# A gated mix of a state-space convolution and segment attention: second half with one PSUM tile per role, transfers on SyncE, reciprocals from SBUF to SBUF, and eight unread products a unit

## The chip, the cores and the metric

The program runs on one core of a Trainium2 chip. The metric is device microseconds (us) of one execution. The engines are TensorE (PE, matmuls; PEld, its weight loads), VectorE (DVE), ScalarE (ACT), GpSimd (POOL) and SyncE (SP, which issues transfers). Each takes its instructions in order and they wait for each other by semaphores. A transfer (DMA) is issued by SP, ACT or POOL, and the issuing engine waits in its own queue until what the transfer needs is ready.

## The reference

Inputs: `A_u` (1 x 2048 x 448), the parameters of a diagonal state-space model for 448 channels with 256 states, four 448 x 448 weights, 16 values `beta`, and a gate vector.

```python
x = A_u
g = sigmoid((x * gate_w).sum(-1, keepdims=True))
# branch a: K[d, l] = 2 Re sum_n C[d,n] exp(A[d,n] dt[d] l); y = causal convolution of u with K by FFT
a = irfft(rfft(u_t, 2 * L) * rfft(K, 2 * L))[:L] + u * D_skip
# branch b: 16 heads of 28, four segments of 512 positions
for s in range(4):
    p = softmax(qs @ ks.T * scale + causal_mask)
    a_dot = p @ vs
    a_mem = (phi(qs) @ M) / (phi(qs) @ z + 1e-6)      # memory of the earlier segments
    o = sigmoid(beta) * a_mem + (1 - sigmoid(beta)) * a_dot
    M, z = M + phi(ks).T @ vs, z + phi(ks).sum()
b = concat(o) @ wo
return g * a + (1 - g) * b
```

All of it is float32.

## The kernel before

**Two halves.** The first half (to about 443 us) makes the convolution's kernel and the projections. It leaves in DRAM the queries and keys of each segment and head group (`QD`, `KD`), the values (`VD`), the memory's numerators and denominators (`AM`, `DM`) and the transform of the input (`GU`). The change does not touch it. The second half, `second_half` at L1219, does the attention and the rest of the convolution together.

**The unit.** A unit `i` is one segment and one group of four heads, 16 in all. It has six rounds (`r` in L1280). Each round steps several generators by one, in an order written out by hand that PE, ACT and DVE keep:

- `ahead`: one step of `maxima` (L982) of unit `i + 2`: PE multiplies queries with keys, 32 rows a head, into a PSUM tile; DVE takes the row maxima of it (two to four reads of 128 to 512 columns). After six steps the maxima are transposed on PE (`ps_m`), negated on ACT (`mn`) and sent by POOL's queue into row 28 of the query tile.
- `w`: one step of `weigh` (L1018) of unit `i`: the logits with keys on the rows, from three products each, into a PSUM tile; ACT takes the exp of it into `PT`. At the end POOL zeroes what lies above the diagonal (`affine_select`, L1045).
- `vals` in round 1: `values` (L1047) of unit `i - 1`: 32 products of `PT` with `V` into the tile `pv`, which ACT copies to `pvs`. Row 28 of each head's 32 is the sum of the weights.
- `cv`, 0.68 of a step per round in units 1 to 12: `convolve` (L568). For each of 16 blocks `m` it goes through `transform` (PE, ACT copies to `ks`, ACT issues two transfers that swap halves of `ks`), `product` (PE, then DVE multiplies twice into `pr`) and `back` (PE, ACT copies to `bs`, ACT issues the store to `BB`).
- `ends`: one step of `seg_end` (L1160) in the rounds other than 1, two a round in all six rounds of unit 13. It starts in round 1 of units 4, 8 and 12, for the segment before.

**The segment end.** `norm` (L1105) collects the sums of the weights from `pvs` into `dn` (four transfers from POOL), `inverse` (L1068) takes the reciprocal on DVE, splits it in a high and a low part `rs`, writes them to a DRAM tile `RD` and reads them back into eight rows of `r8`, both from POOL's queue. Later a product with `k.sel` spreads each row over the 32 partitions of a head, and DVE multiplies `pvs` with it. `recall` (L1086) does the same for the denominators of the memory (`dm`, rows 32 to 40 of `r8`) and scales `am`. `skip` (L1131) loads a block of the input as `xt`, and POOL multiplies it by `dbc` (D_skip) and by `gt` (the gate). The output products of a segment are four groups of four matmuls (`out_mm`), added to `xt` by DVE and stored to `TB`.

**PSUM.** L1587 gives the second half one tile `m`, one `pv`, and three tiles of `a`, each of 128 x 1024. Maxima, weights and every step of the convolution take the next of the three in turn. A new user of a tile waits on PE until the engine that read the last contents is done.

**Unread products.** `turn_over` (L1236) multiplies constants, 128 x 128 by 128 x 512 in bf16, into `pv`. Nobody reads the result. There are three in each of the four rounds ahead of unit 0 and in the six of unit 0, and one beside each of the eight `last` steps of units 14 and 15 (the convolution's final transform, L666).

**Transfers.** `k.dma` (L1412) issues from SP, `k.adma` from ACT, `k.pdma` from POOL. `k.ldma` is `k.dma` placed behind the latest load of `gu`. SP's transfers are ordered by a planner; PE's matmuls keep the order of the program, and `k.dve` and `k.sca` chain DVE's and ACT's.

Of the kernel before, what the change touches and what calls it, by code (L numbers as in the profile page):

```python
# [27 lines left out]
SEG = 512  # L28
# [512 lines left out]
def transform_k(nc, k, fp):  # L541


    k2 = k.kb.rearrange("p b q -> p (b q)")
    gkv = k.GK.rearrange("k r n d -> (k r) n d")
    for i in range(8):
        gs = fp.tile([128, 4, 4, 112], F32, tag="gs", name="gs", bufs=4)
        pts = [k.ps("a") for jj in range(2)]
        for b in range(2):
            o = (32 * b + 4 * i) * 112  # L550
            for j in range(4):
                r = slice(32 * j, 32 * j + 32)
# [12 lines left out]
        yield  # L565


def convolve(nc, k, fp):  # L568
# [31 lines left out]
    def transform(m):  # L600
# [4 lines left out]
        for a in range(2):  # L605
            k.adma(x[a, :, 1], x[1 - a, :, 0])

# [7 lines left out]
    def back(m):  # L615

        pt = k.ps("a")
        w, x = cb[m // 2][:, m % 2], pr.pop(m)
# [27 lines left out]
def finish(nc, k, fp):  # L646
# [19 lines left out]
    def last(wc):  # L666
        ws = slice(2 * wc, 2 * wc + 2)
        py = k.ps("a")
        for w in range(2):
# [277 lines left out]
def attend(nc, k, ap):  # L947
# [34 lines left out]
    def maxima(i):  # L982
# [4 lines left out]
        for b, hp in MSTEPS:  # L987
            pt = k.ps("a")
            for t, o, n in PLACES[b]:
# [28 lines left out]
    def weigh(i):  # L1018
# [3 lines left out]
        for b, hp in STEPS:  # L1022
            pt = k.ps("a")
            for kt, o, n in PLACES[b]:
# [42 lines left out]

    def inverse(x, rows, h0, h1, dst, queue):  # L1068


        f = 16 * (h1 - h0)
        rc = ap.tile([128, 64], F32, tag="rc", name="rc", bufs=1)
        rs = ap.tile([128, 2, 64], F32R, tag="rs", name="rs", bufs=1)
        v.reciprocal(rc[:, :f], x)
        v.tensor_copy(rs[:, 0, :f], rc[:, :f])
        v.tensor_tensor(rs[:, 1, :f], rc[:, :f], rs[:, 0, :f], ALU.subtract)
        rd = k.dr.tile([2, 4, 32 * f], F32, tag=f"RD{f}", name="RD", bufs=2)
        queue(rd.rearrange("b j (i f) -> (j i) b f", f=f), rs[:, :, :f].bitcast(F32))
        queue(
            dst[rows : rows + 8, h0:h1].rearrange("p h q -> p (h q)").bitcast(F32),  # L1080
            rd.rearrange("b j q -> (b j) q"),
        )

    am, r8 = {}, {}

    def recall(s):  # L1086

        am[s] = ap.tile([128, 4, SEG], F32, tag="am", name="am", bufs=1)
        k.ldma(am[s], k.AM[:, :, s - 1].rearrange("h p q -> p h q"))
        dn = ap.tile([128, 64], F32, tag="dm", name="dm", bufs=1)  # L1090
        k.ldma(dn, k.DM[s - 1].rearrange("j h (i f) -> (j h i) f", f=64))
        r8[s] = ap.tile([40, 4, SEG], F32R, tag="r8", name="r8", bufs=1)
        for _ in range(2):
            yield
        v.tensor_scalar(dn, dn, 1e-6, None, ALU.add)
        inverse(dn, 32, 0, 4, r8[s], k.pdma)
        for _ in range(3):
            yield
# [6 lines left out]
    def norm(s, h0, h1, queue):  # L1105

        pvs = pvss[s]
        f = 16 * (h1 - h0)
        dn = ap.tile([128, 64], F32, tag="dn", name="dn", bufs=1)
        for j in range(4):  # L1110
            queue(
                dn[32 * j : 32 * j + 32, :f],
                pvs[32 * j + 28 : 32 * j + 29, h0:h1].rearrange("o h q -> o (h q)").rearrange("o (i f) -> o i f", f=f),
            )
        if s == 0:
            r8[s] = ap.tile([40, 4, SEG], F32R, tag="r8", name="r8", bufs=1)
        for _ in range(2):
            yield
        inverse(dn[:, :f], 0, h0, h1, r8[s], queue)
        for _ in range(3):  # L1120
            yield
        for hg in range(h0, h1):
            o = pvs[:, hg]
# [7 lines left out]
    def skip(s, t):  # L1131

        i = 4 * s + t
        xt = ap.tile([128, D], F32, tag="xt", name="xt", bufs=4)
        k.ldma(xt, k.u[128 * i : 128 * i + 128])
        k.pin(nc.gpsimd.tensor_tensor(xt, xt, k.dbc, ALU.mult))
        k.pin(nc.gpsimd.tensor_scalar(xt, xt, k.gt[:, i : i + 1], None, ALU.mult))
        return xt

# [6 lines left out]
    def skip_last():  # L1146

        for t in range(4):
            xt = skip(3, t)
            i = 12 + t  # L1150
            k.dma(k.TB[128 * i : 128 * i + 128], xt)

    def out_mm(s, t, po, hgs):
# [32 lines left out]
    def last_end(step, vals):  # L1186
# [7 lines left out]
        for _ in range(2):  # L1194
            pt = k.ps("a")
            pos += [pt[:, 0, :D], pt[:, 1, :D]]
# [22 lines left out]
def second_half(nc, k, ap, tp, fp, fin):  # L1219
# [53 lines left out]
    n = 0  # L1273
    for i in range(16):
# [69 lines left out]
def gated_mix(ctx, tc, k):  # L1344
# [297 lines left out]
```

## Time and profile before

| what | value |
|---|---|
| three runs | 857.24, 858.96, 859.09 us, median 858.96 |
| the profiled execution | 861.14 us |
| its span, first to last instruction | 859.4 us |
| mean granted clock of TensorE | 0.899 |
| bytes moved, read and written in DRAM | 88.77 and 60.63 MB, 174 GB/s |

The granted clock is the share of TensorE's full clock that the throttle let through. In this trace it is either 1.0 or 0.5 at a time, and a figure between these is a mean over a stretch. Busy time of PE runs from the first start to the modelled end of pipelined matmuls, so it is an upper bound of what PE did. A row of waits names the engine and tile that waited, the one that ended the wait, the sum in us, the number of times and the longest. A row of a group gives line, engine, operation, tiles (out<-in), shapes and count, then busy us and mean ns, then idle time ahead of it. Most engine work goes through helpers, so the lines L1354 and L1400 stand for many operations and the tile names tell them apart.

### The profile page before, as it was taken

Reading aid. Unit: us, or ns where it says so; the run is one execution under the profiler, and the core shown is the slowest. Engines: PE = TensorE matmul, PEld = TensorE weight load, DVE = VectorE, ACT = ScalarE, POOL = GpSimd, SP = SyncE. Lnnn points to the kernel's source line nnn. Section 1 sums busy time; section 2 is a strip of 40 time slices with the busy share of each in tenths; the row PEclk is TensorE's granted clock in tenths of the full one; section 3 lists DMA queues with packets and bytes.
Section 4 is the critical chain, followed back from the end, with each engine's and each line's share of the span. In section 5 each row is a group of like instructions: output and inputs, shape, how many; then the busy total and the mean of one; then the engine's idle time right before and its main releaser. Section 6 shows DMA issues by size and latency. Waiting matters only on the chain.

```text
span 859.4 us, 18898 instructions
## 1 busy us (share of the span) xinstructions
PE 721.2 (84%) x7583; PEld 393.7 (46%) x7583; DVE 579.7 (67%) x1139; ACT 510.1 (59%) x610; POOL 194.1 (23%) x233
## 2 busy tenths in 40 slices
PE   1687988998889989899989888889887798747897
PEld 1364655764447645466544433334333344313343
DVE  8878678777787777886668745456475657524475
ACT  4876889799997989989852333434243334411220
POOL 5324111001110111101100211171117116711110
PEclk9998999999999989999989867869886797858699
DMA  9347853334633246323569976686558467562684
GB/s 242 93 111 235 241 184 110 98 106 161 207 125 96 93 152 207 132 83 114 195 233 338 358 200 211 221 262 241 179 167 297 129 223 245 196 221 95 162 268 132
DMA packets 90337, 158.22 MB, mean 184 GB/s; under 512 B 20626, under 2 KB 58186, under 8 KB 90202
## 3 DMA queue, kind: packets, MB, share of 16 engines
q1 hardware_dynamic: 78618, 138.74, 50.6%
q10 hardware_dynamic: 9984, 16.52, 5.4%
q0 software_dynamic: 1648, 1.76, 0.7%
q8 instruction: 60, 0.98, 0.5%
q14 instruction: 27, 0.22, 0.1%
HBM read 88.77 MB, written 60.63 MB: 174 GB/s over the span
## 4 chain that ended last, share of the span: by engine, by line
PE 45%; DVE 17%; ACT 16%; DMA 10%; issue 8%; POOL 2%; SPq 1%; ACTq 1%; DVEq 0%; POOLq 0%
PE ps_a L1400 16%; PE ps_m L1400 14%; ACT cs L1354 7%; PE ps_pv L1400 6%; PE ps_arg L1400 4%; DVE jk L1354 4%; PE ps_k L1400 3%; DVE Y L396 3%; ACT L1354 2%; DMA r<-RD 2%; PE ps_m L1403 2%; DVE Y L397 2%; DMA w<-WD 1%; DVE X L392 1%; DMA RD<-rs 1%
## 5 line engine op out<-in xcount | busy, mean ns | idle before, releaser
L1354 ACT ACTIVATE PT<-ps_a 128x1024 f32<-128x1024 f32 (+1 forms) x96 | 84.1, 881 | 155.8 <-PE ps_a L1400 145.7
L1354 DVE CUSTOM_DVE_ANT_0 jk<-ps_a,mk 128x512 f32<-128x512 f32 (+3 forms) x256 | 125.3, 490 | 73.3 <-PE ps_a L1400 64.8
L358 POOL TENSOR_TENSOR EX<-EX,cab 128x1024 f32<-128x1024 f32 x28 | 54.0, 1929 | 307.4 <-ACT EX L1354 286.0
L1354 ACT ACTIVATE cs<-ps_arg 128x1024 f32<-128x1024 f32 x111 | 107.3, 1020 | 2.4 <-DVE Y L397 2.1
L1400 PE MATMUL ps_a<-qu,ku 32*128 32x512 f32 (+3 forms) x768 | 98.6, 379 | 10.0 <-DVE mx L1354 8.1
L1400 PE MATMUL ps_m<-xh,w 112*128 112x512 f32 x256 | 92.8, 412 | 1.9 <-DMA w<-WD 1.9
L1045 POOL TENSOR_SCALAR_AFFINE_SELECT PT<-PT 128x256 f32<-128x256 f32 (+1 forms) x96 | 46.8, 491 | 200.8 <-ACT PT L1354 199.8
L392 DVE TENSOR_TENSOR X<-EX,cs 128x1024 f32<-128x1024 f32 x56 | 70.2, 1254 | 24.3 <-ACT cs L1354 24.1
L1400 PEld LDWEIGHTS ps_a<-qu,ku 32*128 32x128 f32 x768 | 66.5, 206 | 22.3 <-DVE mx L1354 14.3
L1400 PE MATMUL ps_k<-Y,X 128*32 128x64 f32 x3584 | 64.1, 226 | 11.8 <-DVE Y L397 11.8
L1400 PEld LDWEIGHTS ps_k<-Y,X 128*32 128x32 f32 x3584 | 54.9, 113 | 37.4 <-DVE Y L397 20.2
L396 DVE TENSOR_TENSOR Y<-EY,cs 128x1024 f32<-128x1024 f32 x56 | 70.0, 1251 | 0.0
L1354 ACT ACTIVATE cs<-cs,bhp 128x1024 f32<-128x1024 f32 x56 | 64.4, 1151 | 1.8
L1400 PE MATMUL ps_a<-ku,qu 32*128 32x512 f32 (+3 forms) x256 | 49.5, 418 | 14.2 <-DVE mx L1354 7.1
L398 DVE SCALAR_TENSOR_TENSOR Y<-EY,cs 128x512 f32<-128x512 f32 x56 | 39.1, 699 | 31.2 <-ACT cs L1354 30.1
L1354 ACT ACTIVATE EY<-ps_arg 128x1024 f32<-128x1024 f32 x52 | 53.1, 1031 | 10.1 <-PE ps_arg L1400 9.0
L1400 PEld LDWEIGHTS ps_m<-xh,w 112*128 112x128 f32 x256 | 48.0, 188 | 21.0 <-issue 7.9
L1400 PEld LDWEIGHTS ps_a<-ku,qu 32*128 32x128 f32 x256 | 23.7, 198 | 71.9 <-issue 28.8
L1400 PE MATMUL ps_pv<-PT,V 128*32 128x128 f32 (+3 forms) x512 | 51.8, 560 | 0.0
L1400 PE MATMUL ps_arg<-ct,lh 64*128 64x512 bf16 x224 | 43.5, 386 | 8.2 <-ACT cs L1354 5.7
L1400 PE MATMUL ps_m<-xl,w 112*128 112x512 f32 x128 | 50.2, 392 | 0.0
L1354 DVE TENSOR_TENSOR pr<-ps_a,ks 128x896 f32<-128x896 f32 x32 | 33.4, 1085 | 18.8 <-PE ps_a L1400 11.3
(210 smaller groups left out, 1288.6 us busy)
## 6 DMA issues: line engine op xcount, KB each, us to landing
w<-WD SPq DMA_DIRECT2D x32, 448.0 KB, 4.2
qu<-QD SPq DMA_DIRECT2D x16, 512.0 KB, 6.0
ku<-KD SPq DMA_DIRECT2D x16, 512.0 KB, 7.5
GU<-gs SPq DMA_DIRECT2D x32, 224.0 KB, 3.8
GK<-gs SPq DMA_DIRECT2D x8, 896.0 KB, 5.0
gk<-GK SPq DMA_DIRECT2D x16, 448.0 KB, 4.2
gu<-GU SPq DMA_DIRECT2D x16, 448.0 KB, 6.7
ks<-ks ACTq DMA_DIRECT2D x32, 224.0 KB, 4.1
```

The costliest lines, as they stand in the source:

```text
L358: nc.gpsimd.tensor_tensor(o, o, cab, ALU.mult)
L392: v.tensor_tensor(X, ex, t[:, :, 0], ALU.mult)
L396: v.tensor_tensor(Y[:, :, :, :32], lo, y[:, :, :, ::-1], ALU.mult)
L397: v.tensor_tensor(Y[:, 0, :, 32:], ey[:, :, 32:], y[:, 0], ALU.mult)
L398: v.scalar_tensor_tensor(Y[:, 1, :, 32:], ey[:, :, 32:], -1.0, y[:, 1], ALU.mult, ALU.mult)
L1045: nc.gpsimd.affine_select(sl, sl, pat, ALU.is_ge, 0.0, base=0, channel_multiplier=-1)
L1354: x = op(*args, **kw)
L1400: tc.keep_in_program_order(nc.tensor.matmul(*args, **kw))
L1403: tc.keep_in_program_order(nc.tensor.transpose(*args))
```

## The change

- **PSUM**: the three tiles `a` are replaced by one `mx` (maxima), one `w` (weights) and one `c` (convolution). The transform ahead of unit 0 uses `w` and `c`; `last` alternates `c` and `mx`; the final projection takes `w` and `mx`.
- **Queues**: the swap of `ks` and the store of `bs` move from ACT's queue to SP's. `dn` and all transfers of the reciprocals move from POOL's queue to SP's.
- **Reciprocals**: `inverse` has no DRAM tile. Each of the eight rows of `r8` is written by one transfer from 32 partitions of `rs`.
- **Segment end**: the loads and collections of `norm` and `recall` are stepped ahead, the multiplication of `xt` by `gt` goes to ACT and follows its load by a step, ahead of POOL's by `dbc`; `am` is loaded after the last use of its tile and its products come with the last two output groups. In unit 13 two steps a round are taken only from round 2 on. The same work for the last segment (`skip_last`) is spread over units 10 and 11.
- **Unread products**: in units 1 to 15 there is one ahead of rounds 0 and 2 and two ahead of rounds 3, 4 and 5.

```diff
-        pts = [k.ps("a") for jj in range(2)]
+        pts = [k.ps(t) for t in ("w", "c")]
...
-            k.adma(x[a, :, 1], x[1 - a, :, 0])
+            k.dma(x[a, :, 1], x[1 - a, :, 0])
...
-        k.adma(k.BB[4 * m : 4 * m + 4].rearrange("(i s) r n d -> (s r n) i d", i=2), bs)
+        k.dma(k.BB[4 * m : 4 * m + 4].rearrange("(i s) r n d -> (s r n) i d", i=2), bs)
...
-        py = k.ps("a")
+        py = k.ps(("c", "mx")[wc % 2])
...
-            pt = k.ps("a")
+            pt = k.ps("mx")
...
-            pt = k.ps("a")
+            pt = k.ps("w")
...
+    def inverse(x, rows, dst):
+        rc = ap.tile([128, 64], F32, tag="rc", name="rc", bufs=2)
+        rs = ap.tile([128, 2, 64], F32R, tag="rs", name="rs", bufs=2)
+        v.reciprocal(rc, x)
+        v.tensor_copy(rs[:, 0], rc)
+        v.tensor_tensor(rs[:, 1], rc, rs[:, 0], ALU.subtract)
+        for b in range(2):
+            for j in range(4):
+                o = rows + 4 * b + j
+                k.dma(
+                    dst[o : o + 1].rearrange("o h (i f) -> o (h i) f", f=64).bitcast(F32),
+                    rs[32 * j : 32 * j + 32, b].bitcast(F32),
+                )
...
     def recall(s):
+        dn = ap.tile([128, 64], F32, tag="dm", name="dm", bufs=1)
+        k.ldma(dn, k.DM[s - 1].rearrange("j h (i f) -> (j h i) f", f=64))
+        yield
+        v.tensor_scalar(dn, dn, 1e-6, None, ALU.add)
+        inverse(dn, 32, r8[s - 1])
+        yield
         am[s] = ap.tile([128, 4, SEG], F32, tag="am", name="am", bufs=1)
         k.ldma(am[s], k.AM[:, :, s - 1].rearrange("h p q -> p h q"))
+        yield
         for hg in range(4):
             pb = k.ps("m")
-            k.mm(pb, k.sel[32:40], r8[s][32:40, hg], start=True, stop=True)
+            k.mm(pb, k.sel[32:40], r8[s - 1][32:40, hg], start=True, stop=True)
...
+    def scaled(s, t, xt):
+        i = 4 * s + t
+        act(xt, xt, AF.Copy, scale=k.gt[:, i : i + 1])
         k.pin(nc.gpsimd.tensor_tensor(xt, xt, k.dbc, ALU.mult))
-        k.pin(nc.gpsimd.tensor_scalar(xt, xt, k.gt[:, i : i + 1], None, ALU.mult))
...
     def seg_end(s):
         xts = [skip(s, t) for t in range(4)]
-        yield from norm(s, 0, 4, k.pdma)
-        memory = recall(s + 1)
+        sums, memory = norm(s), recall(s + 1)
+        next(sums)
+        next(memory)
+        yield
+        for t in range(2):
+            scaled(s, t, xts[t])
+        yield
+        for t in range(2, 4):
+            scaled(s, t, xts[t])
+        yield
+        next(sums)
+        yield
+        next(memory)
+        yield
+        yield
+        for _ in range(4):
+            next(sums)
+            yield
+        next(memory)
         for t in range(4):
             po = k.ps("m")
             out_mm(s, t, po[:, :D], range(4))
             store(s, t, po[:, :D], xts[t])
-            next(memory)
+            if t > 1:
+                next(memory)
             yield
         yield from memory
...
             else:
+                if r != 1:
+                    turn_over(1 if r < 3 else 2)
                 step(ahead)
                 step(w)
...
-                for _ in range(2 if i == 13 else 1):
+                for _ in range(2 if i == 13 and r > 1 else 1):
...
-            if i == 11 and r == 2:
-                k.skip_last()
+            if i == 10 and r == 2:
+                skips = k.skip_last()
+            if i == 10 and r > 2 or i == 11 and r < 3:
+                step(skips)
...
-            {"m": ([128, 512], 1), "a": ([128, 2, 512], 3), "pv": ([128, 512], 1)},
+            {"m": ([128, 512], 1), "pv": ([128, 512], 1)} | {t: ([128, 2, 512], 1) for t in ("mx", "w", "c")},
```

More of the change, by code (lines that the diff above doesn't have):

```diff
@@ L588, in second @@
     def second(m, x):
-        pt = k.ps("a")
+        pt = k.ps("c")
         w = cf[m // 2]
@@ L615, in back @@
     def back(m):
-        pt = k.ps("a")
+        pt = k.ps("c")
         w, x = cb[m // 2][:, m % 2], pr.pop(m)
@@ L1022, in weigh @@
         for b, hp in STEPS:
-            pt = k.ps("a")
+            pt = k.ps("w")
             for kt, o, n in PLACES[b]:
@@ L1066, in values @@
         yield
[L1068 to L1082, printed above, removed]
+    def inverse(x, rows, dst):
[11 more added lines that the diff above has]
+                )
@@ L1091, in recall @@
[L1091 to L1098, printed above, removed]
+        yield
         for hg in range(4):
             pb = k.ps("m")
-            k.mm(pb, k.sel[32:40], r8[s][32:40, hg], start=True, stop=True)
+            k.mm(pb, k.sel[32:40], r8[s - 1][32:40, hg], start=True, stop=True)
@@ L1102, in recall, with norm @@
             v.scalar_tensor_tensor(am[s][:, hg], am[s][:, hg], k.gh[:, hg : hg + 1], pb, ALU.mult, ALU.mult)
             yield
-    def norm(s, h0, h1, queue):
+    def norm(s):
         pvs = pvss[s]
-        f = 16 * (h1 - h0)
         dn = ap.tile([128, 64], F32, tag="dn", name="dn", bufs=1)
         for j in range(4):
-            queue(
-                dn[32 * j : 32 * j + 32, :f],
-                pvs[32 * j + 28 : 32 * j + 29, h0:h1].rearrange("o h q -> o (h q)").rearrange("o (i f) -> o i f", f=f),
-            )
[L1115 to L1122, printed above, removed]
+            k.dma(
+                dn[32 * j : 32 * j + 32],
+                pvs[32 * j + 28 : 32 * j + 29].rearrange("o h q -> o (h q)").rearrange("o (i f) -> o i f", f=64),
+            )
+        r8[s] = ap.tile([40, 4, SEG], F32R, tag="r8", name="r8", bufs=1)
+        yield
+        inverse(dn, 0, r8[s])
+        yield
+        for hg in range(4):
@@ L1135, in skip @@
         k.ldma(xt, k.u[128 * i : 128 * i + 128])
+        return xt
+    def scaled(s, t, xt):
+        i = 4 * s + t
+        act(xt, xt, AF.Copy, scale=k.gt[:, i : i + 1])
         k.pin(nc.gpsimd.tensor_tensor(xt, xt, k.dbc, ALU.mult))
-        k.pin(nc.gpsimd.tensor_scalar(xt, xt, k.gt[:, i : i + 1], None, ALU.mult))
-        return xt
     def store(s, t, po, xt):
@@ L1146, in skip_last @@
     def skip_last():
-        for t in range(4):
-            xt = skip(3, t)
+        xts = [skip(3, t) for t in range(4)]
+        yield
+        for t, xt in enumerate(xts):
+            scaled(3, t, xt)
             i = 12 + t
             k.dma(k.TB[128 * i : 128 * i + 128], xt)
+            yield
     def out_mm(s, t, po, hgs):
@@ L1161, in seg_end @@
         xts = [skip(s, t) for t in range(4)]
-        yield from norm(s, 0, 4, k.pdma)
-        memory = recall(s + 1)
+        sums, memory = norm(s), recall(s + 1)
[9 more added lines that the diff above has]
+        next(sums)
+        yield
+        next(memory)
+        yield
+        yield
+        for _ in range(4):
+            next(sums)
+            yield
+        next(memory)
         for t in range(4):
@@ L1193, in last_end @@
             yds.append(yd)
-        for _ in range(2):
-            pt = k.ps("a")
+        for t in ("w", "mx"):
+            pt = k.ps(t)
             pos += [pt[:, 0, :D], pt[:, 1, :D]]
```

2 lines of the change are left out of this document (removed).

## The prediction

> **What bounds the kernel now.** I read the page first, then the stretches of the second half, then who made TensorE (PE) wait there.
>
> ```profile
> span 859.4 us, 18898 instructions
> PE 721.2 (84%) x7583; PEld 393.7 (46%) x7583; DVE 579.7 (67%) x1139; ACT 510.1 (59%) x610; POOL 194.1 (23%) x233
> PEclk9998999999999989999989867869886797858699
> PE 45%; DVE 17%; ACT 16%; DMA 10%; issue 8%; POOL 2%; SPq 1%; ACTq 1%; DVEq 0%; POOLq 0%
> ```
>
> PE is the busiest engine and holds the largest share of the chain that ended last. Its granted clock is near full in the left half of the slices and falls to 5 to 8 tenths in the right half, which is what the change touches. The next view cuts that half at the value products (the `pv` groups, one per unit): units 1 to 4, 5 to 8, 9 to 12, unit 13 and the end. Columns: length, busy time of PE, PEld, DVE, ACT and POOL, granted clock, DMA share, GB/s.
>
> ```profile
> 491.60:576.40 84.80, 71.23 (x558) 31.82 (x556) 43.68 (x141) 33.86 (x43) 27.21 (x42) 0.72 0.69 217
> 576.40:665.40 89.00, 76.71 (x610) 34.68 (x612) 52.80 (x161) 33.79 (x43) 28.58 (x44) 0.85 0.67 225
> 665.40:764.40 99.00, 76.16 (x603) 35.36 (x605) 55.21 (x161) 33.08 (x42) 39.11 (x52) 0.79 0.64 215
> 764.40:801.90 37.50, 27.86 (x135) 13.76 (x139) 17.22 (x46) 6.03 (x8) 4.46 (x9) 0.77 0.36 108
> 801.90:859.40 57.50, 51.23 (x294) 21.28 (x294) 33.94 (x45) 11.38 (x15) 6.33 (x13) 0.92 0.64 187
> ```
>
> Two losses show. First, PE is busy but at a reduced clock. If busy time scales with the clock, each stage loses busy x (1 - clock): 71.23 x 0.28 = 19.9, 76.71 x 0.15 = 11.5, 76.16 x 0.21 = 16.0, 27.86 x 0.23 = 6.4 and 51.23 x 0.08 = 4.1, together 57.9 us. Second, PE idles: 84.8 - 71.2 = 13.6 us in the first stage, and much more in the third and fourth. Who it waits for, in total, times, longest:
>
> ```profile
> PE ps_m L1400 <- DMA r<-RD: 20.5, 3, 13.0
> PE ps_a L1400 <- DVE mx L1354: 13.0, 17, 3.5
> PE ps_a L1400 <- DVE pr L1354: 6.2, 5, 2.2
> PE ps_a L1400 <- ACT PT L1354: 3.9, 6, 0.9
> PE ps_m L1400 <- DVE pvs L1354: 3.2, 2, 2.3
> ```
>
> The largest is the transfer of the reciprocals at the segment ends. Around its longest case POOL did this:
>
> ```profile
> 739.64 1.15 POOL L1136 TENSOR_TENSOR xt<-xt,dbc 128x448 f32<-128x448 f32 x1
> ...
> 749.63 1.40 POOL L1137 TENSOR_SCALAR xt<-xt,gt 128x448 f32<-128x448 f32 x1
> 750.99 0.64 POOL L1045 TENSOR_SCALAR_AFFINE_SELECT PT<-PT 128x512 f32<-128x512 f32 x1
> 751.57 0.80 POOL L1078 DMA_DIRECT2D RD<-rs  x1
> 756.79 0.53 POOL L1079 DMA_DIRECT2D r<-RD  x1 [4.42 <-DMA RD<-rs]
> ```
>
> POOL is in order. From 739.64 to 751.03 the multiplications by `dbc` and `gt` stood ahead of the issue at L1078, and then two transfers ran one after the other through DRAM, while PE did nothing for 13.0 us.
>
> **Term A, reciprocals: -18.** The change issues these transfers from SyncE (SP), past POOL's work, and drops the DRAM leg. The landing times (KB each, us to landing) bound the new chain:
>
> ```profile
> RD<-rs POOLq DMA_DIRECT2D x6, 64.0 KB, 3.0
> r<-RD POOLq DMA_DIRECT2D x6, 64.0 KB, 4.6
> dn<-pvs POOLq DMA_DIRECT2D x12, 8.0 KB, 5.5
> xt<-in_A_u SPq DMA_DIRECT2D x16, 224.0 KB, 6.3
> ```
>
> Before: 3.0 + 4.6 plus two issues plus POOL's delay. After: eight issues of one row each and one landing like `dn<-pvs`, the nearest (small, SBUF to SBUF): with an issue at the 0.53 us of L1079 above, 8 x 0.53 + 5.5 = 9.7 us. At least three rounds lie between reciprocal and use; a round is 84.8 / 24 = 3.5 us, so the cover is 10.5. It fits narrowly. At segment 2 the old program stepped twice a round, leaving half of that cover; the new one doubles only from round 2 on. I take 18 of the 20.5; bounds 0 and -20.5.
>
> **Term B, clock: -29.** Eight unread products of the full array per unit are added, in the rounds other than 1. Does that hold the clock? These rows decide (columns as in the stage view):
>
> ```profile
> 474.70:478.10 3.40, 2.48 (x14) 1.01 (x15) 2.96 (x14) 0.58 (x1) 0.00 (x0) 1.00 1.00 402
> 560.00:563.40 3.40, 2.23 (x22) 1.44 (x18) 3.33 (x9) 1.77 (x2) 3.37 (x5) 1.00 0.98 309
> 570.30:573.70 3.40, 3.40 (x24) 1.15 (x16) 1.40 (x4) 1.22 (x2) 3.36 (x4) 0.50 0.94 269
> 589.00:615.00 26.00, 25.93 (x185) 12.13 (x185) 16.48 (x47) 8.38 (x12) 5.20 (x10) 1.00 0.68 235
> 684.00:716.00 32.00, 31.52 (x235) 14.71 (x239) 20.55 (x57) 11.96 (x16) 6.67 (x12) 1.00 0.71 234
> 815.00:855.00 40.00, 38.98 (x223) 16.36 (x219) 27.18 (x38) 7.84 (x11) 4.53 (x9) 1.00 0.70 217
> ```
>
> The three long stretches keep 1.00: there, full-array output products or the last transform mix with the attention products, and PE is busy 97% and more. The first two rows are full-clock stretches with PE 66 to 73% busy, and in both the clock falls right behind them. At 570.3 PE is 100% busy at 0.50: in the cold state the narrow attention and 64x64 products alone don't bring the clock back. So work that fills the gaps with the full array should both delay the fall and hasten the return. But unit 0 already has three products a round, and the first row lies there. I take half of the 57.9; bounds 0 and -50.
>
> The Trainium skill, "TensorE: Matmul & The Clock Gate", section "Why this matters for your kernels", says that the clock falls when PE idles for more than about 3 us. This case's rows disagree: the stretches at 474.7 and 560.0 held 0.9 and 1.2 us of idle in all. By that rule products put into short gaps would bring nothing, which is the first rival.
>
> **Term C, price of the products: +19.** Fifteen units times eight is 120. In unit 0 three in a row moved the next group by this much, at full clock and then at half:
>
> ```profile
> 470.09 0.81 PE L1400 MATMUL ps_pv<-wz 128*128 128x512 bf16 x3
> 470.83 0.50 PE L1400 MATMUL ps_a<-ku,qu 32*128 32x384 f32 x4
> ...
> 478.00 1.39 PE L1400 MATMUL ps_pv<-wz 128*128 128x512 bf16 x3
> 479.31 0.79 PE L1400 MATMUL ps_a<-qu,ku 32*128 32x512 f32 x2
> ```
>
> That is 0.74 / 3 = 0.25 us each at full clock and 1.31 / 3 = 0.44 at half, so 30 us in all, or 52 if everything were cold. Nothing hides it in the dense stretches: 16 products in units 14 and 15 (4.0 us) and, over 26 + 32 = 58 us of about 21 us a unit, 22 more (5.5 us). The other 82 (20.5 us) stand ahead of the maxima, where PE waits for the reads of the last maxima (13.0 us above); I call half hidden, so 4.0 + 5.5 + 10 = 19. Bounds 9.5 and 52. A product also takes the `pv` tile, so the one of round 2 waits for ACT's copy behind the value product, 0.60 us by the row of `pvs` below, under a convolution step in most units.
>
> **Term D, one PSUM tile per role, and the gate on ACT: +5.**
>
> ```profile
> L1354 ACT ACTIVATE PT<-ps_a 128x1024 f32<-128x1024 f32 (+1 forms) x96 | 84.1, 881 | 155.8 <-PE ps_a L1400 145.7
> L1354 DVE CUSTOM_DVE_ANT_0 jk<-ps_a,mk 128x512 f32<-128x512 f32 (+3 forms) x256 | 125.3, 490 | 73.3 <-PE ps_a L1400 64.8
> L1354 ACT ACTIVATE pvs<-ps_pv 128x512 f32<-128x512 f32 x16 | 9.6, 597 | 36.4 <-PE ps_pv L1400 36.4
> ```
>
> Three tiles turned in a ring; now maxima, weights and convolution have one each. The maxima of a round wait for the reads of the round before (two to four of 0.49), the weights for an exp of 0.88 with a maxima group (0.5) and a product or two (0.25 each) ahead of it. In the 68% of rounds with a convolution step both are covered. In the others, about 23 of the 72 rounds of units 1 to 12, some 0.3 us can show: +7 at worst. Against it, PE's 6.2 us on `pr` belong to the shared ring in part. I put the roles at +1 (-6 to +7). The multiplication by `gt` moves to ACT, 16 of about the 0.60 us of `pvs` (the nearest, a copy of 512), on an engine 33.86 / 84.8 = 40% busy; but it comes one round (3.5 us) behind the load of `xt`, which lands in 6.3. ACT is in order, so exps queue behind it and PE behind those: 2.8 us at four places, 11 at worst, 0 if the loads are issued ahead; I take +4. The 48 issues that leave ACT stand on SP; ACT's share of the chain's issue is 1%, so I give that nothing.
>
> The Trainium skill, "DMA: Bandwidth & Descriptors", section "Issuing engines are not separate DMA queues", says that another issuing engine only saves issue time. It would price the move to SP at nothing, and no run here isolates it yet.
>
> **Term E, waits of unit 13: -4.** PE waits 3.2 us there for `pvs`; with fewer doubled rounds this and its neighbours shrink. Bounds 0 and -6.
>
> **Sum.** -18 - 29 + 19 + 5 - 4 = -27. The profiled execution took 861.14 us, 2.2 over the median of 858.96: 861.1 - 27 = 834, or 832 against the median.
>
> **Rivals.**
> 1. The products don't hold the clock (slower). Place: rounds 3 to 5. For it: three a round didn't in unit 0. Against: the 1.00 at 815 with one a round beside the last transform. Then B is -3, and at a clock near 0.8 the products cost 0.32 each, 38, of which I let 4 hide: -18 - 3 + 34 + 5 - 4 = +14, 873. It decides when less than 17 us of the 57.9 come back at that price (34 + 5 - 18 - 4).
> 2. SP becomes the wait. Its queue also is in order:
>
> ```profile
> SPq L1416 <- DVE tb L1354: 31.4, 7, 8.0
> SPq L1416 <- DVE pvs L1354: 21.9, 2, 20.7
> ```
>
> A reciprocal behind such a waiting issue loses its cover of 0.8 us at once. Six chains 1.7 us late on average make A +10: 861.1 + 10 - 29 + 19 + 5 - 4 = 862, 860. Against: the order of emission puts them ahead of `am` and `TB`.
> 3. The single tiles bind: each round shows the read or the exp, D +20: 849, 847.
> 4. More is hidden and held: A -20, B -42, C +12, D 0, E -5: -55, 804.
>
> PE's order is written out by hand, so the products do land where the diff puts them.
>
> **How the numbers follow.** Forecast 0.45, rivals 1 to 4: 0.20, 0.08, 0.15, 0.12. About 0.2% tells this kernel from no change. Forecast, rivals 3 and 4 and a little of 2 give faster 0.73; rival 1 and most of rival 2 give slower 0.24; 0.03 is left between. The likeliest is 832. The range 806 to 870 takes in the forecast with B between -50 and 0, rival 3, rival 2, about half of rival 4 and the lower half of rival 1.
>
> **What would show it.** A: no PE wait for the reciprocals over 2 us; POOL off the chain. B: granted clock near 0.9 in the first three stages. C: 120 more products on `wz`, and PE busy rising by less than 30. D: PE's waits for `mx` and `PT` growing by no more than a few us; ACT waiting for `xt` under 4. The forecast is wrong if the clock in units 1 to 4 stays near 0.72, or if SP's queue shows up ahead of PE in the chain.

## The result, and the profile after

Over 20 runs of each on one chip the changed kernel took 857.47 us in the median (840.52 to 868.72) and the kernel before 864.00 (853.32 to 873.48). The ratio is 0.9865 [0.9825, 0.9905], about 12 us less, where the forecast was 27 less. Here and below a median is of all runs and a ratio only of the fast ones, those within 1.5% of their kernel's fastest, so the two can differ by some us. The profiled execution took 857.84 us and is near the median. The page of it:

```profile
span 855.5 us, 19160 instructions
PE 720.8 (84%) x7678; PEld 393.9 (46%) x7703; DVE 581.3 (68%) x1139; ACT 519.6 (61%) x626; POOL 157.2 (18%) x193
PEclk9998999998989999999996699999999999988999
PE 49%; DVE 17%; ACT 16%; issue 8%; DMA 6%; SPq 2%; POOL 1%; DVEq 0%; ACTq 0%; POOLq 0%
```

The clock is back in the right half, but a dip to 6 has appeared in the middle, at the seam of the halves. DMA's share of the chain fell from 10% to 6%. The stages (columns as in the prediction) show both. The first row of the changed kernel is the head of the second half: the transform ahead of unit 0 and unit 0, up to the first value product.

```profile
447.80:508.40 60.60, 47.05 (x276) 23.09 (x280) 34.26 (x110) 13.94 (x17) 6.58 (x11) 0.75 0.77 277
508.40:583.30 74.90, 61.37 (x586) 27.36 (x588) 43.16 (x145) 36.35 (x47) 18.29 (x32) 0.95 0.72 230
583.30:669.40 86.10, 75.12 (x637) 33.92 (x640) 55.63 (x163) 36.03 (x47) 18.24 (x32) 0.99 0.67 228
669.40:756.80 87.40, 74.37 (x627) 33.87 (x636) 53.95 (x160) 37.45 (x50) 22.71 (x36) 0.97 0.62 208
756.80:795.40 38.60, 29.82 (x145) 13.85 (x146) 16.48 (x43) 6.03 (x8) 3.47 (x7) 0.84 0.48 175
795.40:855.50 60.10, 52.71 (x309) 21.75 (x309) 34.15 (x45) 11.49 (x15) 6.26 (x12) 0.99 0.72 199
```

The head of the kernel before, which the prediction did not show:

```profile
444.20:491.60 47.40, 41.66 (x274) 19.36 (x273) 34.41 (x112) 14.56 (x18) 6.59 (x11) 0.93 0.95 346
```

From the first value product to the end, 367.8 us became 347.1. Split as the prediction does it: the loss by the clock (busy x (1 - clock)) fell from 57.9 to 3.1 + 0.8 + 2.2 + 4.8 + 0.5 = 11.4; idle PE (length - busy) from 64.6 to 53.7; what is left, work at full clock, rose from 245.3 to 282.0. That is -46.5 - 10.9 + 36.7 = -20.7. The head gave 13.2 of it back, 47.4 to 60.6, and it began 3.6 us later, so the span shrank by 3.9 alone. PE's waits in the changed kernel, first in the head (one row), then from the first value product on (engine, what it waited for: total, times, longest):

```profile
PE ps_mx L1423 <- DVE mx L1377: 9.8, 8, 2.5
...
PE ps_mx L1423 <- DVE mx L1377: 17.9, 17, 2.4
PE ps_c L1423 <- DVE pr L1377: 9.5, 5, 3.3
PE ps_m L1423 <- DVE tb L1377: 5.8, 7, 0.8
PE ps_m L1423 <- DVE pvs L1377: 3.8, 2, 2.1
```

The reciprocals are gone from the list (20.5 before). The largest wait is now that of the maxima for their one tile, in the head too, where the kernel before had this row:

```profile
PE ps_a L1400 <- DVE mx L1354: 3.1, 6, 1.1
```

The timeline of the head of the changed kernel, PE's rows and then DVE's (start, length, tile, count, idle time before and its releaser):

```profile
457.78 0.50 PE L1423 MATMUL ps_mx<-ku,qu 32*128 32x512 f32 x2
460.74 0.44 PE L1423 MATMUL ps_mx<-ku,qu 32*128 32x384 f32 x2 [2.46 <-DVE mx L1377]
...
458.26 1.09 DVE L1377 COPY gs<-ps_c 128x896 f32<-128x896 f32 x1 [0.53 <-PE ps_mx L1423]
459.27 0.68 DVE L1377 CUSTOM_DVE_ANT_0 jk<-ps_mx,mk 128x512 f32<-128x512 f32 x1
...
459.99 0.69 DVE L1377 CUSTOM_DVE_ANT_0 jk<-ps_mx,mk 128x512 f32<-128x512 f32 x1
```

In two of the transform's rounds there are two maxima steps, and this is one of them. The second needs the tile of the first, whose two reads stand on DVE behind the transform's copy `gs`. So PE is idle for 2.46 us. The stretches around that place:

```profile
457.80:462.00 4.20, 1.74 (x24) 1.26 (x22) 3.08 (x8) 0.92 (x1) 0.00 (x0) 1.00 1.02 288
462.00:479.00 17.00, 14.09 (x69) 6.73 (x61) 8.22 (x26) 3.63 (x5) 0.00 (x0) 0.50 0.62 248
```

The clock was full up to 462 and half for the 17 us behind it. PE's waits in the two rounds of this kind (2.46 and 1.84 us) are 4.3 of the head's 9.8; the rest stand in the four rounds ahead of unit 0 and in unit 0, where little work lies between two uses of the tile.

Behind the head the waits look like this (PE's rows, unit 3):

```profile
539.42 0.50 PE L1423 MATMUL ps_mx<-ku,qu 32*128 32x512 f32 x2
539.43 0.97 PE L1423 MATMUL ps_w<-qu,ku 32*128 32x512 f32 x6
542.79 0.50 PE L1423 MATMUL ps_mx<-ku,qu 32*128 32x512 f32 x2 [2.40 <-DVE mx L1377]
```

Between two uses of the tile stands only a group of weights, no step of the convolution. That is so for 16 of the 17 waits, 17.3 of the 17.9 us.

### The profile page after: what moved, and what is told of

It is laid out like the page before. It is cut to its first block, busy times and chain, and to the rows that moved or that the text cites. A ratio compares the mean times of both kernels' runs of the same rounds, so it can differ in the third digit from the quotient of the medians.

```text
span 855.5 us, 19160 instructions
## 1 busy us (share of the span) xinstructions
PE 720.8 (84%) x7678; PEld 393.9 (46%) x7703; DVE 581.3 (68%) x1139; ACT 519.6 (61%) x626; POOL 157.2 (18%) x193
## 3 DMA queue, kind: packets, MB, share of 16 engines
q10 hardware_dynamic: 3072, 1.84, 0.8%
## 4 chain that ended last, share of the span: by engine, by line
PE 49%; DVE 17%; ACT 16%; issue 8%; DMA 6%; SPq 2%; POOL 1%; DVEq 0%; ACTq 0%; POOLq 0%
PE ps_m L1423 15%; PE ps_pv L1423 8%; PE ps_c L1423 7%; ACT cs L1377 7%; PE ps_w L1423 6%; DVE jk L1377 6%; PE ps_mx L1423 5%; PE ps_arg L1423 4%; PE ps_k L1423 3%; DVE Y L396 2%; ACT L1377 2%; PE ps_m L1426 2%; DVE pr L1377 2%; DVE Y L397 1%; DMA winv<-in_B_wv 1%
## 5 line engine op out<-in xcount | busy, mean ns | idle before, releaser
L1377 DVE CUSTOM_DVE_ANT_0 jk<-ps_mx,mk 128x512 f32<-128x512 f32 (+3 forms) x256 | 125.4, 490 | 81.5 <-PE ps_mx L1423 72.7
L1377 ACT ACTIVATE PT<-ps_w 128x1024 f32<-128x1024 f32 (+1 forms) x96 | 84.6, 881 | 151.5 <-PE ps_w L1423 150.7
L1423 PE MATMUL ps_w<-qu,ku 32*128 32x512 f32 (+3 forms) x768 | 87.1, 344 | 2.8 <-ACT PT L1377 2.5
L1423 PE MATMUL ps_mx<-ku,qu 32*128 32x512 f32 (+3 forms) x256 | 47.6, 409 | 30.1 <-DVE mx L1377 27.7
L1423 PEld LDWEIGHTS ps_w<-qu,ku 32*128 32x128 f32 x768 | 60.0, 186 | 13.2 <-issue 6.1
L1377 ACT ACTIVATE EY<-ps_arg 128x1024 f32<-128x1024 f32 x52 | 53.2, 1030 | 12.9 <-PE ps_arg L1423 11.8
L1423 PEld LDWEIGHTS ps_mx<-ku,qu 32*128 32x128 f32 x256 | 22.6, 193 | 70.6 <-DVE mx L1377 51.9
L1423 PE MATMUL ps_pv<-wz 128*128 128x512 bf16 x137 | 48.4, 407 | 3.6 <-ACT pvs L1377 3.1
L1423 PEld LDWEIGHTS <-lh 64*128 64x128 bf16 x392 | 21.8, 95 | 51.2 <-issue 38.6
```

The lines of the kernel that those rows point to most:

```text
L1377: x = op(*args, **kw)
L1423: tc.keep_in_program_order(nc.tensor.matmul(*args, **kw))
```

## The experiments

The first theory was that the single tile for the maxima costs the head its 13 us and the rest went about as forecast. Against it stood chance, the unread products and the queues; later theories are in the expectations. All ratios are to the kernel before, timed on the same chip, with 95% intervals.

**The changed kernel again.** No edit.

> The changed kernel once more, for a second profile. Theory 1 (single tiles slow the head): from the first product of the convolution kernel's transform to the first value products it takes 58 to 61 us again, against 47 before, and the whole is 0.98 to 0.99 of the time before. Rival (the head was slow by chance, through the clock): 47 to 52 us in this profile.

857.75 us, 0.9902 [0.9858, 0.9947]. The head took 59.3 us, and PE waited 9.8 us there for the maxima once more. The long head is no accident of one execution, and neither are the stages behind it: cut at the value products again, they took 76.4, 88.2, 86.6, 37.7 and 60.2 us, at clocks of 0.93, 0.96, 0.98, 0.86 and 0.99, with 17.4 us of waits for the maxima.

**Without the products.**

```diff
-                if r != 1:
-                    turn_over(1 if r < 3 else 2)
```

> The changed kernel without the 120 unread products of units 1 to 15. Theory 1 (the products hold the clock and are paid in full): the granted clock of units 1 to 12 falls from 0.97 to 0.70 to 0.85, PE work falls by some 30 us, and the time stays within 8 us of the changed kernel, 0.98 to 1.00 of before. Rival a (something else of the redesign holds the clock): the clock stays above 0.93 and the time falls by 25 to 30 us, 0.955 to 0.965. Rival b (the products are what made the kernel faster): 1.01 or more.

863.56 us, 0.9986 [0.9944, 1.0028]. The head and units 1 to 12 of this kernel:

```profile
445.60:502.60 57.00, 42.93 (x273) 20.79 (x273) 34.49 (x112) 13.94 (x17) 6.58 (x11) 0.83 0.80 295
502.60:766.70 264.10, 220.53 (x1758) 100.93 (x1756) 152.27 (x462) 109.25 (x144) 59.21 (x100) 0.80 0.62 208
766.70:802.70 36.00, 26.77 (x138) 13.13 (x140) 16.94 (x45) 6.03 (x8) 3.56 (x7) 0.86 0.50 186
802.70:859.00 56.30, 48.39 (x296) 21.03 (x294) 34.35 (x45) 11.49 (x15) 5.96 (x12) 0.99 0.72 213
```

The long head is there without the products, so they are not its cause. Behind it the clock is 0.80 again. By the same split as above, with units 1 to 12 as one stretch, this kernel has 247.4 of work, 48.3 of clock loss and 60.7 of idle from the first value product on, together 356.4. So the products added 34.6 of work (0.29 each), brought back 36.9 of clock and 7.0 of idle: -9.3. Cut into the same five stretches it gives 33.2, 35.5 and 7.0, so the first two are good to about 1.5 us.

**The tiles in turn in the head only.** From unit 1 on each role has its own tile, as in the changed kernel.

```diff
+    ring = itertools.cycle(("w", "c", "mx"))
+    k.tag = lambda role: next(ring)
...
-            pt = k.ps("mx")
+            pt = k.ps(k.tag("mx"))
...
+        if i > 0:
+            k.tag = lambda role: role
```

> The changed kernel with the three big PSUM tiles used in turn until the end of unit 0, and by role from unit 1 on. Theory 1: the head takes 46 to 49 us as before, the whole 10 to 14 us less than the changed kernel, 0.970 to 0.978 of before. Rival (the head was slow by chance): no difference from the changed kernel, 0.985 to 0.99.

847.67 us, 0.9821 [0.9777, 0.9866]. Head and units 1 to 12:

```profile
443.90:493.90 50.00, 43.35 (x274) 20.52 (x274) 34.95 (x112) 14.01 (x17) 6.58 (x11) 0.89 0.90 335
493.90:742.60 248.70, 214.21 (x1854) 95.23 (x1852) 151.52 (x463) 109.81 (x144) 59.23 (x100) 0.97 0.66 222
```

The head is 50.0, 2.6 of it a wait for `ku`, and units 1 to 12 stay at the 248.4 of the changed kernel. Over all profiles the head is 57.0 to 60.6 in the three kernels with single tiles there, and 45.8 to 55.9, mean 49, in the rest. The gain is 4 to 7 us by the ratios (against 0.9865, and against the 0.9902 of the same chip), less than the 10 to 14 expected.

**The kernel before with the products.** The two lines that the second experiment removed, put into the old rounds.

> The kernel before with the 120 unread products alone. Theory 1: granted clock 0.95 or more in units 1 to 12, the waits for the reciprocals stay at about 20 us, PE work grows by 30 us or more, the time is 0.985 to 1.005 of before. Rival (only together with the single tiles do the products hold the clock): the clock stays under 0.88 and the time is 1.015 or more.

863.72 us, 0.9988 [0.9955, 1.0021]. In the old kernel the products are worth nothing. The profile is of an execution of 852.45 us, 11 under the median, so its stages are not compared. The wait for the reciprocals is still there (12.9 us in that one), and the clock of units 1 to 12 is 0.93 in it, so the products raise the clock here too.

**Three tiles in turn everywhere**, the rest as changed.

```diff
-    ... {t: ([128, 2, 512], 1) for t in ("mx", "w", "c")}
+    ... "a": ([128, 2, 512], 3)
```

> The changed kernel with the ring of three PSUM tiles kept everywhere, all else as changed, products included. Theory 2 (a tile per role costs PE idle time in the units too, because it waits for VectorE's reads one step earlier): idle time of PE from the first value products to the end falls from 53 to 40 to 46 us, the head is 46 to 49 us, and the whole is 8 to 12 us faster than the kernel with the ring in the head alone: 0.965 to 0.975 of before. Rival (in the units the roles cost nothing): the same as the ring in the head alone, 0.980 to 0.985.

838.83 us, 0.9685 [0.9647, 0.9724]: the 27 us of the forecast. Head, units 1 to 12, unit 13 and end, then PE's waits for the maxima in the head and, from 508 us on, those for `pr` and the maxima:

```profile
441.70:493.40 51.70, 47.14 (x275) 22.47 (x275) 35.18 (x113) 14.01 (x17) 6.58 (x11) 0.80 0.87 326
493.40:737.90 244.50, 216.63 (x1854) 97.16 (x1852) 152.28 (x462) 109.82 (x144) 59.27 (x100) 0.97 0.68 225
737.90:777.20 39.30, 32.31 (x143) 14.66 (x141) 16.43 (x43) 5.52 (x8) 3.07 (x6) 0.76 0.46 170
777.20:840.70 63.50, 57.26 (x311) 22.57 (x309) 34.96 (x46) 11.89 (x16) 6.37 (x13) 0.90 0.66 189
...
PE ps_a L1423 <- DVE mx L1377: 1.4, 3, 0.8
...
PE ps_a L1423 <- DVE pr L1377: 12.3, 9, 3.5
PE ps_a L1423 <- DVE mx L1377: 6.8, 11, 1.4
```

In the head the idle time is 51.7 - 47.1 = 4.6 against 60.6 - 47.1 = 13.5, with as low a clock (0.80 and 0.75). So what the ring gives back in this head is the waits, 8.9 us. The low clock is not typical of a ring: over all profiles the head idles 12.5 to 14.1 us with single tiles and 4.5 to 7.7 without, and its clock is 0.75 to 0.83 against 0.89 or more in eleven of the other thirteen. From the first value product on, idle is 41.1 instead of 53.7, but in this execution the clock lost 20.0 instead of 11.6, mostly in unit 13 and the end, and the stretch is as long (347.3) as in the changed kernel.

**The same without the products.** The second experiment's edit in the ring.

> The ring everywhere and no added products: what is left of the change are the transfers on SyncE, the reciprocals from SBUF to SBUF and the new order of the segment ends. Theory 2: the waits for the reciprocals are gone and nothing else has come in their place: idle time from the first value products on falls from 64 to 42 to 48 us, cold time stays, 0.975 to 0.985 of before. Rival (the waits come back in another place of the segment ends, at the output products): idle 55 or more, 0.99 to 1.0.

851.48 us, 0.9842 [0.9804, 0.9881]. The products are worth 13 us in the ring by the medians (851.48 - 838.83). The rest of the redesign alone is worth 1.6%, some 14 us; idle time from the first value product on is 48.9 us in its profile, 64.6 before. Units 1 to 12 went back to a clock of 0.79:

```profile
490.30:753.60 263.30, 228.51 (x1762) 104.24 (x1760) 152.07 (x464) 109.51 (x144) 59.30 (x100) 0.79 0.63 211
```

**Fewer products, tiles in turn in the head.** First none in units 6, 10, 14 and 15, then four a unit (rounds 2 to 5, one each).

```diff
-                if r != 1:
+                if r != 1 and i not in (6, 10, 14, 15):
```

> Ring in the head, and no added products in units 6, 10, 14 and 15, where output products or the last transform keep TensorE dense. Theory 1 (products are paid in full where the clock holds without them): PE work falls by 8 to 9 us, the clock stays at 0.97 or more in units 5 to 12, the time falls by 6 to 9 us against the ring in the head with all products: 0.972 to 0.977 of before. Rival (they hold the clock there too): cold time grows by 8 us or more and the time stays.

850.34 us, 0.9817 [0.9765, 0.9869], as with all of them, so the expected gain did not come. In the profile (855.93 us, 6 over the median) the clock of units 5 to 8 and 9 to 12 is 0.94 and 0.88, where the kernel with all products has 1.00 and 0.96: it looks like the rival, that the products hold the clock in those units too.

```diff
-                if r != 1:
-                    turn_over(1 if r < 3 else 2)
+                if r > 1:
+                    turn_over(1)
```

> Ring in the head, and four products a unit in place of eight (one in each of rounds 2 to 5). Theory 1: the clock needs about eight: with four, cold time in units 1 to 12 is halfway between none (44 us) and eight (8 us), PE work is 17 us less, the time within 4 us of that with eight, 0.978 to 0.987 of before. Rival (four are enough): cold time under 14 us and the time 10 us or more lower, 0.970.

859.32 us, 0.9904 [0.9866, 0.9943], worse than eight (0.9821) and just outside of what was expected. Units 1 to 12 of it:

```profile
488.40:747.90 259.50, 219.63 (x1806) 98.94 (x1804) 151.97 (x464) 109.24 (x144) 59.16 (x100) 0.89 0.64 214
```

The clock lies between the 0.80 of none and the 0.97 of eight, and the stretch is 11 us longer than with eight (248.7).

**Products in units 0 to 12 only**, in the ring: `if r != 1 and i < 13`.

> The ring everywhere, and the eight products only in units 1 to 12. Theory 1 (products are paid in full where the clock holds anyway): unit 13 takes 35 to 36 us in place of 39 and the end 55 to 57 in place of 63.5, as without products; units 1 to 12 as with them. The whole is 8 to 12 us less than the ring with products in all units: 0.955 to 0.962 of before. Rival (without them the clock falls in units 13 to 15): 0.968 or more.

834.51 us, 0.9683 [0.9632, 0.9734]. In the profiles unit 13 took 35.0 us instead of 39.3 and the end 56.4 instead of 63.5, at a clock no lower (0.81 and 0.97 against 0.76 and 0.90), so there the products cost and return nothing. But units 1 to 12 took 249.9 us instead of 244.5, at a lower clock (0.94 against 0.97) though nothing was changed in them, and the ratio is the same as with all products. The 8 to 12 us that were expected did not come; a gain of this edit alone isn't settled.

**The 48 issues back on ACT**, in the ring: `k.adma` for the swaps of `ks` and the stores of `bs`.

> The ring everywhere with products in all units, and the swaps of ks and the stores of bs issued from ScalarE's queue again. Theory (moving these 48 issues is worth nothing either way): 0.965 to 0.972, the same as the ring. Rival (SyncE's queue delays them, or ScalarE's time matters): a change of 4 us or more.

851.30 us, 0.9875 [0.9831, 0.9920], 16 us worse by the ratios than with these issues on SP (0.9685), 12 by the medians, which are of two chips. Units 1 to 4 took 83.8 us; in the ring with SP 73.4. In the last of the four, from the timeline:

```profile
566.12 0.92 ACT L1377 ACTIVATE ks<-ps_a 128x896 f32<-128x896 f32 x1
567.26 4.99 SPq L1439 DMA_DIRECT2D r<-rs  x8
570.77 1.15 ACTq L606 DMA_DIRECT2D ks<-ks  x2
572.02 1.02 ACT L1377 ACTIVATE PT<-ps_a 128x1024 f32<-128x1024 f32 x1 [4.99 <-issue]
573.10 1.65 PE L1423 MATMUL ps_a<-qu,ku 32*128 32x512 f32 x6 [3.35 <-ACT PT L1377]
```

ACT's `ks` was done at 567.04, but the issue of its swap stands at 570.77, while SP put out eight issues of reciprocals from 567.26 on. ACT is in order, so the exp waited 4.99 us and PE 3.35. The granted clock was 1.00 up to 570.5 and 0.50 from 571.0 on, so it fell about 1 us into PE's wait:

```profile
569.70:573.10 3.40, 0.05 (x3) 0.00 (x1) 3.30 (x8) 1.02 (x1) 0.00 (x0) 0.66 0.47 160
573.10:576.00 2.90, 2.90 (x14) 1.22 (x18) 0.61 (x2) 1.02 (x1) 0.53 (x2) 0.50 0.58 198
```

This place doesn't explain the whole. By units, the 10.4 us are 3.9, 2.0, 1.3 and 3.1, and only the last unit has a burst of SP in it. The first, here and in the ring with SP, differs by its clock:

```profile
490.85:513.19 22.34, 21.00 (x140) 8.60 (x138) 9.98 (x34) 8.67 (x11) 3.08 (x6) 0.65 0.66 179
493.39:511.82 18.43, 16.01 (x140) 6.88 (x138) 9.36 (x33) 8.71 (x11) 3.47 (x7) 0.90 0.59 165
```

What lowered it there isn't known; a single profile of each can't tell it from chance.

**Which role must not have its own tile.** Both with the tiles in turn in the head, and two tiles in turn for two of the roles from unit 1 on: first the weights alone, then the maxima alone.

```diff
+            k.tag = lambda role: role if role == "w" else next(pair)
```

> Ring of three until the end of unit 0; from unit 1 on the weights keep a tile of their own, and the maxima and the convolution take two in turn; products in all units. Theory 3 (it is the maxima's own tile that costs, since PE comes to it before VectorE has read the last contents): PE's waits for the maxima's reads fall from 18 to 20 us to 8 to 12, and the time is near the ring's, 0.968 to 0.974. Rival (it is the weights' own tile): 0.980 or more, as with a tile each.

843.36 us (833.36 to 853.82), 0.9699 [0.9642, 0.9757].

> As the run before, but the maxima keep a tile of their own, and the weights and the convolution take two in turn. Theory 3: no better than a tile each, 0.979 to 0.985, waits for the maxima's reads at 18 us or more. Rival: near the ring, 0.968 to 0.974.

860.63 us, 0.9959 [0.9924, 0.9994]. PE's waits from 508 us on for the maxima, first with the weights alone (on either of the two tiles), then with the maxima alone, where the wait for `rest` stands below:

```profile
PE ps_mx L1428 <- DVE mx L1382: 1.4, 3, 0.7
...
PE ps_c L1428 <- DVE mx L1382: 0.9, 1, 0.9
```

```profile
PE ps_mx L1428 <- DVE mx L1382: 15.6, 16, 2.4
PE ps_c L1428 <- DVE rest L1382: 6.7, 4, 3.0
```

2.3 us against 15.6. Two tiles in turn for maxima and convolution are no worse than three for all, as far as the intervals tell (0.9699 and 0.9685). The second kernel is worse than forecast, and worse than the one with a tile per role (0.9821). In it the final transform shares tiles with the weights (`rest`, 6.7 us), and its end took 73.3 us, where it took 60.1 and 63.7 with a tile per role, so its ratio is not a price for the maxima alone. The two profiles are 10 and 6 us under the medians of their kernels.

**The old kernel, products, and the 48 issues on SP.**

> The kernel before with the 120 products, and with the swaps of ks and the stores of bs issued from SyncE; reciprocals and PSUM as before. Theory 4 (a transfer's issue on ScalarE's queue holds up the exp behind it, PE waits and the clock falls, which is what the products are paid to prevent): the move brings 8 to 14 us here as in the ring, 0.983 to 0.990 of before, and PE waits under 2 us for PT. Rival (the move is worth something only beside the new segment ends, whose multiplications by gt load ScalarE): 0.995 to 1.0, as the old kernel with products alone.

862.50 us, 0.9969 [0.9929, 1.0009], against 0.9988 with them on ACT: nothing. There the reciprocals go by POOL's queue, and SP has no burst for the issues to meet. PE's wait for them stays (18.1 us, once 13.1). Split as above, the profile (863.89 us) has 280.7 of work, 32.4 of clock loss and 56.9 of idle from the first value product on, where the kernel before has 245.3, 57.9 and 64.6: the products held the clock here as well, and their work took all of it.

**The best of it.** Weights alone, the other two in turn, products up to unit 12.

> A tile of their own for the weights, two in turn for maxima and convolution, ring of three until the end of unit 0, and products only in units 1 to 12. If both findings add up: units 1 to 12 in 238 to 243 us, unit 13 in 35 to 36, the end in 55 to 57, and 0.955 to 0.963 of before. If not: 0.968 to 0.970, as the ring with products to unit 12.

830.71 us (824.02 to 838.79), 0.9614 [0.9555, 0.9672], the lowest ratio of all and 22 to 25 us under the changed kernel by the ratios (0.9865 and 0.9902). Units 1 to 12 took 242.7 us in the profile, unit 13 36.6 and the end 57.0, so the two findings add up about as expected.

## Why the prediction was right or wrong

**The step that failed is term D**: "I put the roles at +1 (-6 to +7)". The ring with all else changed is at 0.9685, the changed kernel at 0.9865: the single tiles cost 16 us, or 19 with the second set of runs of the changed kernel (0.9902, on the ring's chip). Two things were wrong in it.

First, it counted rounds of units 1 to 12 alone. The head, where the same tiles serve the transform and two maxima steps share a round, was not priced. It grew by 13.2 us: idle time went from 47.4 - 41.7 = 5.7 to 13.5, and the clock from 0.93 to 0.75. Tiles in turn there alone bring back 4 to 7 us by the ratios. In every profile without single tiles there the idle time is back to 4.5 to 7.7 us, and in most the clock too (0.89 with the ring in the head alone, but 0.80 with the full ring).

Second, it mis-sized the rounds without a convolution step. That the reads are covered where there is such a step held: all but one of the 17 waits (0.55 us) lie in the other rounds. The term gave those about 23 rounds 0.3 us each. PE waited in 16 of them, 1.1 us on the mean and up to 2.4, as in the rows of unit 3 above: 17.9 us in all, though the products stand ahead of many, against 6.8 in the ring with the products. The weights, which the term priced at the same place, did no harm: 2.2 us on `PT`. The credit for `pr` was there, but small: 9.5 us against the 12.3 of the ring. It is a weaker form of rival 3, which had the read or the exp show in every round, at 847. How much of the 16 to 19 lies here, apart from the head, stays open: tiles in turn in the head alone against the full ring say 12 us by the ratios and 9 by the medians, while in their profiles idle time fell from 50.5 to 41.1 us and the stretch only by 5.0, since the clock lost more.

**With D at its measured size the sum holds.** Without the single tiles the forecast of -27 came out, at 0.9685. That is in part luck, since its terms held less well one by one: A and E together came to about -14 instead of -22, and the 4 us of D's gate that did not appear and a net of B and C that was 3 us better made up for it. It also takes the move of the 48 issues, which the sum put at nothing: with them on ACT the ring is at 0.9875.

**A, reciprocals, -18: the mechanism was right.** No wait of PE on them is left and POOL's share of the chain is 1%. Eight issues took 5 us and a transfer landed in 1.9 (the estimate was 9.7 together):

```profile
580.52 5.01 SPq L1439 DMA_DIRECT2D r<-rs  x8
...
DMA to landing us min/median/max: 1.9/1.9/4.7
```

As time it was worth less. Everything but the products and the single tiles made 1.6%, about 14 us, where A and E together said 22: in that kernel PE's wait for `tb` is 5.3 us (1.1 before), and that for `pr` grew from 6.2 to 11.5.

**B, clock, -29, and C, products, +19: each too small, their net right.** B came to -46.5 over the whole change; the products alone brought 36.9 back. C was 34.6 of work with 7.0 of idle hidden, where 30 and about 10 were assumed. The net of -10 measured -9.3 in the profiles with single tiles, 13 by the medians in the ring. "PE busy up by less than 30" said nothing: busy time hardly moved (721.2 to 720.8), because the work that came was offset by the clock that came back. The rule of the Trainium skill that the prediction weighed ("TensorE: Matmul & The Clock Gate", "Why this matters for your kernels": idle gaps over about 3 us lower the clock) fits neither place shown above: the clock fell behind 2.46 us of idle time in the head, and about 1 us into the 3.35 us beside the burst. And products did raise the clock of units 1 to 12 from 0.80 to 0.97, where PE's longest waits without them were 3.5 and 3.0 us and idle PE went only from 43.6 to 37.5 us in all. Rival 1 is refuted. What is true in it is the count: with four a unit the clock is 0.89.

**D's gate on ACT, +4: it did not appear.** ACT's multiplications and those who waited for them:

```profile
L1377 ACT ACTIVATE xt<-xt,gt x16: 655/658/672, 574.0 to 750.6; 128x448 f32<-128x448 f32 x16
...
  POOL xt L1136: 8.2, 6
  ACT bs L1377: 0.9, 1
```

ACT itself stood for no load; POOL's waiting is off the path.

**E, unit 13, -4: wrong.** It took 38.6 us instead of 37.5. PE waits 3.8 us on `pvs` as before, and without products the unit takes 35.0 to 36.6: what the fewer steps saved, the products took. That PE idles "much more" there than in the first stage was a misreading: in us it is less, 9.6 (37.5 - 27.9) against 13.6, and only the share is larger.

**"The 48 issues that leave ACT ... I give that nothing."** In the old kernel with the products that holds; beside the new segment ends it is worth 12 to 16 us in the ring. The rule cited there (the Trainium skill, "DMA: Bandwidth & Descriptors", "Issuing engines are not separate DMA queues": another issuing engine saves the issue time, usually small) agrees with the first. The second is not small, though it is less than the 48 issues took on ACT in that run, some 22 us by their medians (32 x 0.512 + 16 x 0.366). That SP's burst held ACT's issue, and with it the exp queued behind, fits the times at one place, and the absence of an effect where SP has no burst; it was not tested by itself, and it covers 3 of the 10 us that units 1 to 4 lost. The rest is a lower clock ahead of any burst and stays open. Rival 2 did not occur: SP's queue has 2% of the chain.

**The start of the head** lies at 445.6 to 447.8 us in the three kernels with single tiles there and at 440.8 to 445.0 in the others, though the first half is the same. Most of that is there before the second half begins: its last products of `macc` stand at 431.1 us in the changed kernel, at 426.8 in the ring and at 429.0 with the ring in the head alone. Why isn't known, and in a comparison of single profiles it adds up to 6 us to the price of the single tiles.

## What to carry to other kernels

A ring of buffers and a buffer per role hold the same bytes, but with one buffer a role waits for its own last reader each time, and the place that hurts is where the role comes back with little other work between: look for it in every stage that uses the tiles, also ahead of the loop that the change is about. Filler products can hold the clock, but their own work is paid: here they paid in units 1 to 12, and in unit 13 and the end the profiles show only their cost, so they are placed by stage. A part that is worth nothing in the old kernel (the products, and the move of the issues beside them) can be worth 12 us or more in the new one, so the parts are measured in the new kernel, by taking them out.

## What the runs showed that was not expected

The clock fell behind an idle time of 2.46 us and stayed at 0.50 for 17 us with PE busy 83% of them (14.09 of 17.00). Eight products a unit held 0.97 in units 1 to 12, though PE's array was full with them for only about 8 x 0.29 = 2.3 us of some 21 a unit. An issue on ACT's queue stood for 3.7 us (567.04 to 570.77) while SP issued eight small transfers of 0.6 us each. And the runs of the changed kernel spread over 3% (840.52 to 868.72 us), and a single profile can lie 5 to 11 us off the median of its kernel.
